# Gated attention then top-1 experts on one core: gates in polar form by scans over time, 96-deep heads, state kept in PSUM, routing by batch into fixed places

## The chip, the cores and the metric

The kernel runs on one NeuronCore of a Trainium2 chip. The metric is device time in microseconds (us), the median of the timed runs. A profiled execution gives, beside it, a span (first to last instruction) and the rows by engine: PE (matrix products), PEld (its weight loads), DVE (VectorE), ACT (ScalarE), POOL (GpSimd), SP (which only issues transfers here).

## What is computed

Two blocks follow each other, all in fp32. The first is a linear attention with a complex gate for each of B = 4 batches, H = 8 heads, S = 768 tokens, head size D = 48; the second sends each of the 3072 tokens to one of 8 experts.

```python
mag = np.sqrt(a_re * a_re + a_im * a_im)
scale = np.minimum(mag, 0.999) / (mag + 1e-06)
a_re_n, a_im_n = (a_re * scale, a_im * scale)
...
for t in range(S):
    new_re = ar * S_re - ai * S_im
    new_im = ar * S_im + ai * S_re
    kv = np.einsum('bhd,bhe->bhde', k[:, :, t], v[:, :, t])
    S_re, S_im = (new_re + kv, new_im)
    y[:, :, t] = np.einsum('bhd,bhde->bhe', q[:, :, t], S_re)
...
logits = x @ w_gate
expert_idx = np.argmax(logits, axis=1)
...
    h = np.maximum(xe @ w1[e], 0.0)
    ye = h @ w2[e]
    out[mask] = gate_w[mask, None] * ye
```

x is y with the heads side by side, 384 wide; w1 is 384 x 1024 and w2 1024 x 384 for each expert; `gate_w` is the softmax probability of the chosen expert.

## The kernel before

**Attention.** The running product P of the gates turns the recurrence into products of matrices: a score is the sum over d of (qP) times (kP / |P|^2) over both parts, within chunks of 128 tokens, and a state carries the rest from chunk to chunk. The work is cut into 16 head pairs (4 batches of 4 pairs), two heads in partitions 0-47 and 64-111, all 768 tokens in the free dimension. For each pair `front` (L217) does `limit` (L72: magnitude by Square and Sqrt on ACT, a reciprocal on DVE), `running` (L104: products within blocks of 8 tokens by 28 DVE instructions, then across 16 blocks by 24 more, then six POOL multiplies, adds and subtracts of 720 elements a partition, L138 to L141) and `factors` (L143: a second reciprocal and the two products qp and kp). `attention` (L160) then makes, per chunk and head, the scores (L170, two 48-deep products, one per part), the mask (L174, DVE), the values (L184) and the part of the state (L187); the new state needs a transpose of kp (L192), a copy on ACT (L194), a product (L198) and four DVE instructions (L202 or L204 to L211). DVE helpers all go by L47.

The order is program order: `ready = front(i + 1)` is issued ahead of `attention(i, ...)` in the loop at L232, so that each engine's queue holds the next pair's gates ahead of this pair's products. After a batch, its rows go to HBM (L237) and their logits are made (L240).

**Check and routing.** L244 to L308 test whether any chunk's product is too small, and hold two loops that run zero times with ordinary gates. L310 to L430 then find, for all 3072 tokens at once, the token of each place in 31 tiles of 128 tokens, each of one expert (`NTILE`).

**Experts.** The loop at L444 gathers for each of the 31 tiles its tokens (L446) and the two weight matrices of its expert (L448, L450) by indirect transfers from POOL, 3.1 MB of weights a tile; then three transposes (L453), 24 products of 128 columns (L460), Relu halves on ACT and DVE (L462, L463), 8 products of 384 columns (L466), the scaling (L468, DVE) and an indirect store of the rows (L469, POOL).

Of the kernel before, what the change touches and what calls it, by code (L numbers as in the profile page):

```python
# [19 lines left out]
C = S // 128            # chunks of 128 tokens in a sequence  # L20
HP = H // 2             # head pairs in a batch
NP = B * HP             # head pairs; head u of a pair lies in partitions 64u..64u+63
HS = (slice(0, 64), slice(64, 128))
HD = (slice(0, D), slice(64, 64 + D))
BK = 8                  # tokens in a block of the running product
NB = 128 // BK
NT = N // 128
DT, FT = DM // 128, F // 128
NTILE = NT + E - 1      # tiles of one expert each: sum of ceil(count / 128) is at most this
W = DM + 1              # a row of x and its gate  # L30
TB = 8                  # tokens in a step of the general path
LEAST = 1e-20           # of |product of a chunk's gates|^2, for the factored form
# [3 lines left out]
def gateloop_then_moe(ctx, tc, q, k, a_re, a_im, v, wg, w1, w2, out):  # L36
    nc = tc.nc
    x_hbm = nc.dram_tensor("x_hbm", (N + 1, W), FP32, kind="Internal").ap()

    consts = ctx.enter_context(tc.tile_pool(name="consts", bufs=1))  # L40
    route = ctx.enter_context(tc.tile_pool(name="route", bufs=1))
# [7 lines left out]
    ident = consts.tile([128, 128], FP32, name="ident")  # L49
    make_identity(nc, ident)  # L50
    causal = consts.tile([128, 128], FP32, name="causal")
    make_upper_triangular(nc, causal, val=1.0, diag=True)
    wgate = consts.tile([128, DT * E], FP32, name="wgate")
    nc.sync.dma_start(wgate, wg)
    zrow = consts.tile([1, W], FP32, name="zrow")
    nc.vector.memset(zrow, 0.0)
    nc.sync.dma_start(x_hbm[N:N + 1, :], zrow)

    lg_all = route.tile([128, NT, E], FP32, name="lg_all")
    good = route.tile([128, NP, C], FP32, name="good")  # L60

    def logits(x, tp_pool, tp_tag, lg, xt_pool):
        """x: 128 tokens' rows; their logits into lg (PSUM)."""
        tp = tp_pool.tile([128, DT, 128], FP32, name="xt_ps", tag=tp_tag)
        for d in range(DT):
            nc.tensor.transpose(tp[:, d, :], x[:, d * 128:d * 128 + 128], ident)
        xt = xt_pool.tile([128, DT, 128], FP32, name="xt")
        nc.scalar.copy(xt, tp)
        for d in range(DT):
            nc.tensor.matmul(lg, lhsT=xt[:, d, :], rhs=wgate[:, d * E:d * E + E], start=(d == 0), stop=(d == DT - 1))  # L70

    def limit(a, sq, mag, den):  # L72
        """Gates a: [128, (re, im), n], in place."""
        nc.scalar.activation(sq, a, func=ACT.Square)
        tt(mag, sq[:, 0, :], sq[:, 1, :], ALU.add)
        nc.scalar.activation(mag, mag, func=ACT.Sqrt)
        nc.vector.tensor_scalar_add(den, mag, 1e-6)
        nc.vector.reciprocal(den, den)  # L78
        nc.vector.scalar_tensor_tensor(out=den, in0=mag, scalar=0.999, in1=den, op0=ALU.min, op1=ALU.mult)
        tt(a, a, bc(den[:, None, :], list(a.shape)), ALU.mult)  # L80

    with ExitStack() as att:
        pool = lambda nm, n, **kw: att.enter_context(tc.tile_pool(name=nm, bufs=n, **kw))
        ld = pool("ld", 3)
        bt = pool("bt", 2)
        big = pool("big", 2)
        tmp = pool("tmp", 1)
        small = pool("small", 2)
        psA = pool("psA", 2, space=PSUM)
        psY = pool("psY", 1, space=PSUM)  # L90
        psT = pool("psT", 1, space=PSUM)
        psG = pool("psG", 1, space=PSUM)

        def load(i):
            a = ld.tile([128, 2, S], FP32, name="a", bufs=4)
            nc.sync.dma_start(a[:, 0, :], a_re[i])
            nc.sync.dma_start(a[:, 1, :], a_im[i])
            qs = ld.tile([128, S], FP32, name="qs")
            ks = ld.tile([128, S], FP32, name="ks")
            nc.sync.dma_start(qs, q[i])  # L100
            nc.sync.dma_start(ks, k[i])
            return a, qs, ks

        def running(a):  # L104
            """In place: products of the gates from each chunk's start to each of its tokens."""
            blk = a.rearrange("p u (n j) -> p u n j", j=BK)
            nb = S // BK
            for j in range(1, BK):
                cur = blk[:, :, :, j]
                u = small.tile([128, 2, nb], FP32, name="u")  # L110
                w = small.tile([128, 2, nb], FP32, name="w")
                tt(u, cur, bc(blk[:, 0:1, :, j - 1], [128, 2, nb]), ALU.mult)
                tt(w, cur, bc(blk[:, 1:2, :, j - 1], [128, 2, nb]), ALU.mult)
                tt(cur[:, 0, :], u[:, 0, :], w[:, 1, :], ALU.subtract)
                tt(cur[:, 1, :], u[:, 1, :], w[:, 0, :], ALU.add)
            t = small.tile([128, 2, nb], FP32, name="t")
            nc.vector.tensor_copy(t, blk[:, :, :, BK - 1])
            m = 1
            while m < NB:
                g = nb // (2 * m)  # L120
                tv = t.rearrange("p u (g r m) -> p u g r m", r=2, m=m)
                prod = {}
                for x in range(2):
                    for y in range(2):
                        z = small.tile([128, nb // 2], FP32, name=f"z{x}{y}").rearrange("p (g m) -> p g m", m=m)
                        tt(z, tv[:, x, :, 1, :], bc(tv[:, y, :, 0, m - 1:m], [128, g, m]), ALU.mult)
                        prod[x, y] = z
                tt(tv[:, 0, :, 1, :], prod[0, 0], prod[1, 1], ALU.subtract)
                tt(tv[:, 1, :, 1, :], prod[0, 1], prod[1, 0], ALU.add)
                m *= 2  # L130
            av = a.rearrange("p u (c n j) -> p u c n j", c=C, j=BK)[:, :, :, 1:, :]
            pv = t.rearrange("p u (c n) -> p u c n", c=C)[:, :, :, :NB - 1]
            shape = [128, C, NB - 1, BK]
            prod = {}
            for x in range(2):
                for y in range(2):
                    z = tmp.tile(shape, FP32, name=f"y{x}{y}")
                    tt(z, av[:, x], bc(pv[:, y, :, :, None], shape), ALU.mult, nc.gpsimd)  # L138
                    prod[x, y] = z
            tt(av[:, 0], prod[0, 0], prod[1, 1], ALU.subtract, nc.gpsimd)  # L140
            tt(av[:, 1], prod[0, 1], prod[1, 0], ALU.add, nc.gpsimd)  # L141

        def factors(i, p, qs, ks):  # L143
            """q P and k P / |P|^2, so that a score is the sum over d of both their parts' products."""
            sq = tmp.tile([128, 2, S], FP32, name="sq", bufs=2)
            nc.scalar.activation(sq, p, func=ACT.Square)
# [13 lines left out]
        def attention(i, p, qp, kp, vb, xb):  # L160
# [3 lines left out]
            for half in range(2):  # L164
# [11 lines left out]
                for cc in range(3):  # L176
# [11 lines left out]
                    if c == C - 1:  # L188
                        continue
# [322 lines left out]
```

## Time and profile before

| | us |
|---|---|
| median of 3 runs (1226.98 to 1228.46) | 1227.65 |
| span of the profiled execution | 1230.5 |
| PE busy in it, 4913 instructions | 912.9 |
| DVE busy, 1564 instructions | 766.0 |
| POOL busy, 237 instructions | 267.4 |
| ACT busy, 219 instructions | 132.6 |

The profile is of an execution of its own, whose only time is its span; all three timed runs lie 2 to 3.5 us below it. A row of a table of groups reads: line, engine, operation, output<-input, partitions x elements, count, then busy us and mean ns of one, then the idle time of the engine ahead of it and what ended that. In a table of stretches each engine's busy us stands with its number of instructions in brackets. The granted clock of TensorE is full nearly throughout, so PE durations compare directly.

### The profile page before, as it was taken

How to read it: one execution, taken by the hardware profiler on the slowest of the kernel's cores; microseconds unless marked ns; L12 is line 12 of the kernel's file. 1: busy time of each engine (PE TensorE's matmuls, PEld its weight loads, DVE VectorE, ACT ScalarE, POOL GpSimd, SP SyncE). 2: the span in 40 equal slices, each digit the busy share in tenths (PEclk: the TensorE clock that was granted, in tenths of full speed). 3: DMA queues.
4: the chain of work that ended last, by engine and by line, in shares of the span. 5: the costliest groups of instructions: out<-in, count | busy, mean ns of one | idle time of the engine just before them, and what ended most of it. 6: DMA issues, size and time to landing. Idle time of an engine off the chain costs nothing. (4 is left out here: it accounts for less than half of the span.)

```text
span 1230.5 us, 12763 instructions
## 1 busy us (share of the span) xinstructions
PE 912.9 (74%) x4913; PEld 737.9 (60%) x4913; DVE 766.0 (62%) x1564; ACT 132.6 (11%) x219; POOL 267.4 (22%) x237
## 2 busy tenths in 40 slices
PE   0286585785775886857779558572899999999998
PEld 0165474674654665645657457562677777777776
DVE  6689899789898879998969889514111111111111
ACT  1111101111101121011020110110000000000000
POOL 0220220202202202112022021101233332433330
PEclk9999999999999999999999999999999999999999
DMA  7010100301101121011020000011877878888880
GB/s 256 26 39 14 52 21 31 129 1 52 39 14 52 32 97 39 14 52 39 13 89 1 0 1 1 1 40 18 360 289 301 335 297 327 330 318 322 322 308 6
DMA packets 31682, 143.84 MB, mean 117 GB/s; under 512 B 6689, under 2 KB 12866, under 8 KB 23682
## 3 DMA queue, kind: packets, MB, share of 16 engines
q0 software_dynamic: 12896, 108.36, 23.1%
q1 hardware_dynamic: 12498, 29.90, 7.3%
q10 hardware_dynamic: 6224, 4.73, 1.2%
q8 instruction: 39, 0.64, 0.2%
q14 instruction: 25, 0.20, 0.0%
HBM read 133.52 MB, written 10.83 MB: 117 GB/s over the span
## 5 line engine op out<-in xcount | busy, mean ns | idle before, releaser
L170 PE MATMUL at<-qp,kp 48*128 48x128 f32 x768 | 127.7, 451 | 206.7 <-DVE kp L47 206.7
L170 PEld LDWEIGHTS at<-qp,kp 48*128 48x128 f32 x768 | 104.1, 320 | 226.1 <-DVE kp L47 208.9
L47 POOL TENSOR_TENSOR y<-a,t 128x720 f32<-128x720 f32 x64 | 89.9, 1436 | 626.4 <-issue 594.8
L187 PE MATMUL y<-st,qp 48*128 48x48 f32 x640 | 180.8, 421 | 27.5 <-DVE st L211 22.7
L187 PEld LDWEIGHTS y<-st,qp 48*128 48x128 f32 x640 | 150.5, 317 | 52.4 <-DVE st L211 27.6
L460 PEld LDWEIGHTS h_ps<-xt,w1t 128*128 128x128 f32 x1488 | 173.7, 194 | 13.0 <-issue 5.0
L460 PE MATMUL h_ps<-xt,w1t 128*128 128x128 f32 x1488 | 174.0, 278 | 4.6 <-DMA w1t<-in_moe_w_dram,widx 4.6
L466 PE MATMUL o_ps<-w2t,ht 128*128 128x384 f32 x496 | 167.9, 492 | 12.4 <-ACT ht L462 11.4
L466 PEld LDWEIGHTS o_ps<-w2t,ht 128*128 128x128 f32 x496 | 91.7, 190 | 76.0 <-ACT ht L462 17.3
L184 PE MATMUL y<-vb,am 128*128 128x48 f32 x384 | 122.1, 426 | 5.2 <-DVE am L47 5.2
L455 DVE COPY xt<-xt_ps 128x384 f32<-128x384 f32 x31 | 17.2, 556 | 153.7 <-PE xt_ps L453 153.7
L184 PEld LDWEIGHTS y<-vb,am 128*128 128x128 f32 x384 | 95.2, 313 | 23.6 <-DVE am L47 7.1
L468 DVE TENSOR_SCALAR yo<-o_ps,xs 128x384 f32<-128x384 f32 x31 | 19.2, 618 | 133.5 <-PE o_ps L466 133.5
L152 DVE RECIPROCAL n<-n 128x768 f32<-128x768 f32 x16 | 79.3, 4953 | 0.5
L78 DVE RECIPROCAL den<-den 128x768 f32<-128x768 f32 x16 | 79.2, 4948 | 0.1
L469 POOL DMA_INDIRECT out_dram<-yo,idx x31 | 31.5, 1016 | 198.7 <-DVE yo L468 197.8
L194 ACT COPY kt<-kt_ps 128x256 f32<-128x256 f32 x80 | 29.8, 372 | 321.8 <-PE kt_ps L192 187.7
L198 PE MATMUL g<-vb,kt 128*64 128x48 f32 x640 | 62.3, 316 | 0.5 <-ACT kt L194 0.5
L192 PE MATMUL kt_ps<-ident,kp 128*128 128x128 f32 x160 | 55.4, 448 | 8.1 <-ACT kt L194 8.1
L211 DVE SCALAR_TENSOR_TENSOR st<-s,a,m 128x48 f32<-128x48 f32 x80 | 61.4, 767 | 0.0
L209 DVE SCALAR_TENSOR_TENSOR st<-s,a,m 128x48 f32<-128x48 f32 x80 | 59.7, 746 | 1.2
L462 ACT ACTIVATE ht<-h_ps 128x512 f32<-128x512 f32 x31 | 18.5, 597 | 361.4 <-PE h_ps L460 314.6
(116 smaller groups left out, 972.0 us busy)
## 6 DMA issues: line engine op xcount, KB each, us to landing
a<-in_a_re_dram SPq DMA_DIRECT2D x16, 384.0 KB, 3.0
a<-in_a_im_dram SPq DMA_DIRECT2D x16, 384.0 KB, 3.8
qs<-in_q_dram SPq DMA_DIRECT2D x16, 384.0 KB, 3.8
ks<-in_k_dram SPq DMA_DIRECT2D x16, 384.0 KB, 3.0
vb<-in_v_dram SPq DMA_DIRECT2D x4, 1152.0 KB, 9.4
x_hbm<-xb ACTq DMA_DIRECT2D x4, 1152.0 KB, 8.6
xs<-x_hbm,idx POOLq DMA_INDIRECT x31
w1t<-in_moe_w_dram,widx POOLq DMA_INDIRECT x31
```

Source lines behind the costliest of these rows:

```text
L47: (eng or nc.vector).tensor_tensor(out=o, in0=a, in1=b, op=op)
L78: nc.vector.reciprocal(den, den)
L152: nc.vector.reciprocal(n2, n2)
L170: nc.tensor.matmul(at[:, h, cc * 128:cc * 128 + 128], lhsT=kp[HD[h], u, sl], rhs=qp[HD[h], u, sl], start=(u == 0), stop=(u == 1))
L184: nc.tensor.matmul(yh, lhsT=am[:, h, cc, :], rhs=val(h), start=True, stop=(c == 0))
L187: nc.tensor.matmul(yh, lhsT=qp[HD[h], u, sl], rhs=st[HD[h], u, :], start=False, stop=(u == 1))
L192: nc.tensor.transpose(kt_ps[:, u, :], kp[:, u, sl], ident)
L198: nc.tensor.matmul(g[HS[h], u, :], lhsT=kt[:, u, HS[h]], rhs=val(h), start=True, stop=True)
L209: nc.vector.scalar_tensor_tensor(out=st[:, 0, :], in0=s0[:, 1, :], scalar=end[1], in1=m[:, 0, :], op0=ALU.mult, op1=ALU.add)
L211: nc.vector.scalar_tensor_tensor(out=st[:, 1, :], in0=s0[:, 0, :], scalar=end[1], in1=m[:, 1, :], op0=ALU.mult, op1=ALU.subtract, reverse1 ...
L460: nc.tensor.matmul(h_ps[:, f, :], lhsT=w1t[:, c:c + 128], rhs=xt[:, d, :], start=(d == 0), stop=(d == DT - 1))
L466: nc.tensor.matmul(o_ps, lhsT=ht[:, f, :], rhs=w2t[:, f * DM:f * DM + DM], start=(f == 0), stop=(f == FT - 1))
```

## The change

Nearly all of the kernel is written anew.

- **Gates.** The inputs are laid out with 128 partitions x 3 groups (all 8 heads of 48 fill 384 rows exactly) by tokens. A *unit* is 384 tokens of one batch, so 1152 elements a partition (the first half of batch 0 is two smaller units of 128 and 256 tokens). The log of the gate's magnitude and its angle are found by Ln, Exp and Arctan on ACT and summed over time by `tensor_tensor_scan` on DVE; Exp and Sin of the sums, times q and k, give qp and kp. Both reciprocals and the block products go. Six multiplies of a unit stand on POOL.
- **96-deep heads.** Transfers from SBUF to SBUF (20 a unit, issued by SP) place a head's real and imaginary rows under each other, so that a score is one 96-deep product.
- **State.** The gates are not rescaled at each chunk, so the state is one sum in a PSUM bank (`ST`), to which each chunk adds; DVE copies it to SBUF after each chunk. Outputs are made transposed (`YT`, two heads in two halves of the output partitions), copied by ACT and turned back with the gate's weights beside (`XT`), which also gives the logits.
- **Routing** is done after each batch: every expert has 448 places in HBM (`xs_hbm`), and POOL stores the rows there by indirect transfers of 128.
- **Experts** run one by one: weights loaded once by SP, 448 columns at a time, and the last 64 places of two experts share one output.
- **Order.** `Plan` takes every step with its engine, an assumed duration and its reads and writes, plays it forward, and the steps are emitted in order of their planned start. Each engine's queue keeps that order. Its engines are taken as independent of each other.
- **Check.** Four tests (angle, decay of a chunk, decay in all, places of an expert) set the counts of the two loops, which now come after the experts.

The core of the gates, of a unit (`fast` is the first unit only; left out after Arctan are three scans of the angle, a tensor_scalar, a scalar_tensor_tensor and a tensor_scalar, all on DVE):

```diff
+            activ(a, a, ACT.Ln, (A,), (A,), "LE", n)
+            activ(c, a, ACT.Exp, (A,), (Ck,), "LE", n, scale=-1.0)
...
+                P.add("POOL", pool_t(n), lambda: tt(im, im, c, ALU.mult, nc.gpsimd), (Bk, Ck), (Bk,))
+            P.add("DVE", dve2(n), lambda: nc.vector.tensor_tensor_reduce(
+                out=c, in0=im, in1=im, scale=1.0, scalar=0.0, op0=ALU.mult, op1=ALU.max, accum_out=chk[:, u:u + 1]),
...
+            activ(c, c, ACT.Ln, (Ck,), (Ck,), "LE", n, bias=one)
+            P.add("DVE", dve2(n), lambda: nc.vector.scalar_tensor_tensor(
+                out=a, in0=c, scalar=0.5, in1=a, op0=ALU.mult, op1=ALU.add), (Ck, A), (A,))
+            activ(c, a, ACT.Exp, (A,), (Ck,), "LE", n, scale=-1.0)
+            activ(c, c, ACT.Ln, (Ck,), (Ck,), "LE", n, scale=1e-6, bias=one)
+            P.add("DVE", dve1(n), lambda: nc.vector.tensor_scalar_min(a, a, LNMAX), (A,), (A,))
+            for g in range(G):
+                P.add("DVE", 2 * T * 0.00104 + 0.08, lambda g=g: nc.vector.tensor_tensor_scan(
+                    d[:, g, :], a[:, g, :], c[:, g, :], lend[:, b, g, c0:c0 + 1], ALU.add, ALU.subtract),
...
+            activ(a, d, ACT.Exp, Dk, (A,), "LE", n, bias=cpos)
+            activ(c, d, ACT.Exp, Dk, (Ck,), "LE", n, scale=-1.0, bias=cneg)
...
+                P.add("POOL", pool_t(n), lambda: tt(qq, qq, a, ALU.mult, nc.gpsimd), (Q, A), (Q,))
+                P.add("POOL", pool_t(n), lambda: tt(kk, kk, c, ALU.mult, nc.gpsimd), (K, Ck), (K,))
+            activ(im, im, ACT.Arctan, (Bk,), (Bk,), "T", n)
...
+            activ(si, si, ACT.Sin, Sk, Sk, "T", n, scale=TWOPI)
+            activ(co, co, ACT.Sin, ("co",), ("co",), "T", n, scale=-TWOPI, bias=hpi)
+            for nm, o, x, xk, eng in (("kp", kp, kk, K, "DVE"), ("qp", qp, qq, Q, "POOL")):
+                for part, key, tr in ((1, Sk, si), (0, ("co",), co)):
+                    e = "DVE" if fast else eng
+                    if nm == "kp" and part == 0 and not fast:
+                        e = "POOL"
```

A chunk and the experts (PE parts):

```diff
+                        nc.tensor.matmul(SC[hf][:, (h % 4) * 128:(h % 4) * 128 + 128], lhsT=hk[slot][:, h, o],
+                                         rhs=hq[slot][:, h, o], start=True, stop=True)
...
+                        nc.tensor.matmul(YT[ps, (h // 2) * 128:(h // 2) * 128 + 128], lhsT=V[:, cl, h * 64:h * 64 + 64],
+                                         rhs=am[2 * par + hf][:, h % 4, :], start=(c == 0 and h < 2), stop=True,
...
+                        nc.tensor.matmul(HB[hb][:, 0:CAP], lhsT=w1b[ws][:, c:c + 128], rhs=xrt[s][:, d, :], start=(d == 0), stop=(d == DT - 1))
...
+                            nc.tensor.matmul(OB[ob][64 * z:64 * z + 64, 0:DM], lhsT=ht[z][:, f_, 384:CAP],
+                                             rhs=w2b[(e - 1 + z) % NW][:, f_ * DM:f_ * DM + DM], start=(f_ == 0), stop=(f_ == FT - 1),
```

## The prediction

> **What bounds the kernel now.** I read the stages first, in the table of stretches cut at the first attention product (54 us), the last pair's kp (786), routing (838) and the experts (866 to 1226).
>
> ```profile
> 0.00:54.00 54.00, 0.00 (x0) 0.00 (x0) 33.77 (x67) 8.59 (x7) 10.05 (x14) 1.00 0.45 158
> 54.00:786.00 732.00, 520.19 (x2592) 425.83 (x2592) 654.13 (x1322) 98.43 (x166) 134.65 (x90) 1.00 0.10 35
> 786.00:838.00 52.00, 43.45 (x218) 36.14 (x218) 8.07 (x30) 5.43 (x13) 1.60 (x4) 1.00 0.07 24
> 838.00:866.00 28.00, 2.87 (x30) 2.21 (x30) 15.33 (x55) 1.65 (x2) 7.80 (x13) 1.00 0.29 88
> 866.00:1226.00 360.00, 346.42 (x2074) 273.67 (x2074) 54.19 (x92) 18.51 (x31) 112.35 (x116) 1.00 0.77 295
> ```
>
> Column three after the stretch is DVE: 654 of 732 us, so DVE sets the attention's pace (48.8 us a head pair); in the experts PE does, 346 of 360. In between, 80 us have one engine or none at work. Then the groups and the timeline gave durations:
>
> ```profile
> L460 PE MATMUL h_ps<-xt,w1t 128*128 128x128 f32 x1488 | 174.0, 278 | 4.6 <-DMA w1t<-in_moe_w_dram,widx 4.6
> L466 PE MATMUL o_ps<-w2t,ht 128*128 128x384 f32 x496 | 167.9, 492 | 12.4 <-ACT ht L462 11.4
> L152 DVE RECIPROCAL n<-n 128x768 f32<-128x768 f32 x16 | 79.3, 4953 | 0.5
> L47 POOL TENSOR_TENSOR y<-a,t 128x720 f32<-128x720 f32 x64 | 89.9, 1436 | 626.4 <-issue 594.8
> ```
>
> Last, why DVE is 89% busy with ever fewer elements: its timeline, and POOL's, in one burst of POOL.
>
> ```profile
> 124.95 0.25 DVE L47 TENSOR_TENSOR s<-g,st 128x96 f32<-128x96 f32 x1
> 125.24 1.32 DVE L207 TENSOR_SCALAR m<-s,a 128x96 f32<-128x96 f32 x1
> 126.59 1.36 DVE L209 SCALAR_TENSOR_TENSOR st<-s,a,m 128x48 f32<-128x48 f32 x1
> 127.87 1.47 DVE L211 SCALAR_TENSOR_TENSOR st<-s,a,m 128x48 f32<-128x48 f32 x1
> 129.45 0.26 DVE L47 TENSOR_TENSOR s<-g,st 128x96 f32<-128x96 f32 x1
> 129.74 1.00 DVE L207 TENSOR_SCALAR m<-s,a 128x96 f32<-128x96 f32 x1
> ```
>
> ```profile
> 125.05 5.62 POOL L47 TENSOR_TENSOR y<-a,t 128x720 f32<-128x720 f32 x4 [38.21 <-issue]
> 130.75 3.36 POOL L47 TENSOR_TENSOR a<-y,y 128x720 f32<-128x720 f32 x2
> ```
>
> L207, L209 and L211 take 0.27 us elsewhere; beside POOL each lasts until a POOL multiply ends. The sum at L47 that reads PSUM (0.25) is not held. DVE's "busy" there is waiting.
>
> [...] Here two L184 instructions between 48-deep ones take 0.59 us, against 0.112 each in the experts; parallel halves are shown by nothing.
>
> **Experts.** Durations from start to start. Last-but-one tile: 48 instructions of L460 from 1202.80 to 1208.16, so 0.112 for 128 columns; 16 of L466 from 1209.01 to 1214.27, so 0.329 for 384, 0.856 ns a column. An fp32 product is two instructions. Per expert: 48 of 448 columns at 0.384 = 18.4 us; three full places of 128, 3 x 5.26 = 15.8; 12 transposes at 0.11 to 0.16, 1.6; together 35.8, times 8 = 286. The shared last places: 4 x 32 instructions x 0.329 = 42 if the halves go one after another, 21 if side by side; I take 26. Stalls: a tile's 11.47 us holds 0.5 beyond its PE work; 0.5 at each of 8 experts, 4. Sum **316 us** (307 to 332), for 360 now. Weights fall from 31 to 8 loads of 3.1 MB, hidden under 39 us of products each; bare, one costs 8.5 us at 372 GB/s (the store of x at 820 us, with rows of 1536 bytes).
>
> **Attention: the shared port.** Per unit of 1152 elements, DVE instructions with two SBUF inputs: 4 at 1.35 (0.947 at 768, 1.75 at 1536) = 5.4; one-input ones, 3 at 0.76 (0.559 at 768, halves per element) = 2.3; 6 scans of 384, at half the rate of such an instruction 0.95, at its full rate 0.55: I take 0.95, 5.7; two small copies 0.3. Sum 13.7 (11.3). POOL's six multiplies: 1.436 at 720 gives 2.30 each, 13.8; the slower form at L140 (1.699) would make 16.3. Together 27.5 us of port (25 to 30), for 8 units' worth **220 us** (201 to 240). [...]
>
> DVE's other work reads PSUM and needs no port: per chunk two masks of 512 at 0.67, state copy 0.68, x copy 0.56, logits 0.2 = 2.8, times 24 = 67; routing some 14 small steps of 0.2, times 4 = 11. Of 78, 11 belong to the tail below. Of the other 67, those hide that stand at the head of DVE's queue while a POOL multiply runs: with some 15 of them and 15 port instructions a unit in mixed order, one or two get through before a port instruction stops the queue, so 48 multiplies x 1.5 x 0.6 = 43. I take two thirds, 45, as hidden and add the rest, **22** (0 if all hide, 67 if none). POOL also gets 24 indirect stores at 1.0 in its queue; 18 lie before the tail and fit into its idle half, 18 more at worst.
>
> Everything else lies beneath. ACT: 10 functions at 1.17, copies 3 x 1.55, two table loads at 1.3 = 19 us a unit, 152. PE per chunk: 8 transposes, 16 score, 32 value and state instructions of 128 columns, 16 of 64, 8 of 104, at 0.112 or less: 6.8 to 8.6[...]; I take 8.3, 200 in all (182 to 245). Transfers: 5.5 MB a unit, a fill of 5.5 and stores of 4.7, 54 MB, 146 us at 372 GB/s[...]. SP: 25 issues a unit at 0.4, 10 us. If the port's cover went, ACT or PE would be next, near 200.
>
> **Ends.** Lead-in: inputs land at 4 to 6 us, the first chain has little beside it: 10. From the last gate product to the first expert product: transfer 4, three chunks x 8.3 = 25, routing 14 steps x 0.3 = 4, six indirect stores at 1.3 apart = 8, landing 2.3 (857 to 860 for a gather), load 3.8, transposes and copies 2: **49**. All of now's 80 us between stages goes with that. After the last product: 4.5 as now; the two empty loops, hidden before (trips at 819.3, PE on at 824.8), are bare now, 5.5: **10**.
>
> Sum: 10 + 220 + 22 + 49 + 316 + 10 = 627 us of span. Now's span is 2.9 above its median; I take 3 off: **624 us**.
>
> **The rivals.** *Engines free of each other* (20%): plans and queues happen to set POOL apart from DVE, or the lock holds less for long instructions. Then DVE's own 13.7 + 8.4 + 1.4 = 23.5 a unit binds: 178 after the tail's share, in place of 242: 560. Against it: six rows held to POOL's very end. *The order does not fit* (18%): the plan counts no lock, so late qp and kp stand in front of other work in SP's and PE's in-order queues. Ten us more a unit: 704. For it: one queue issues both the moves and the next loads; against it: double buffers. *Slower* (1.5%): a test sends the kernel into the token loop, bare at the end. 768 tokens at 10 us at least (some 20 DVE steps at 0.33 and a transfer in and out of 3) add 7.7 ms; it decides once, say, one expert has over 448 tokens. Computed from the inputs, the fullest has 421, the decay sums to -79.6 (limit -100), the angle's squared tangent is 0.28 (2.25). That the change does not do what it says would show so too.
>
> **Numbers.** Forecast 60% (585 to 680). From 560 to 705 about one in ten is left out on each side: half of the first rival, half of the second. Within 0.2% (2.5 us, about what a measurement can tell from no change) would need 600 us of errors: 0.5%.
>
> **What would show it.** DVE instructions on SBUF of 1152 elements lasting well over 1.35 us with a POOL multiply beside, some 30 us a unit; scans near 0.95; expert products at 0.384; some 49 us between the last gate product and the first expert product. Multiplies on both engines at bare durations at once would make it wrong, as would PE busy over 90% in the attention, or an expert beyond 41 us.

## The result, and the profile after

The median is **685.9 us** (683.2 to 689.7, four runs) against 1227.3 for the kernel before on the same chip: a ratio of 0.559, 95% interval 0.557 to 0.561. The profiled execution has a span of 685.5. I cut it at the points of the prediction's sum: POOL's first multiply (39.05), the end of the last gate product (294.35), the first expert product (364.11), the last one's end (669.8). The tail has a further cut at 334, when TensorE has finished the attention. Of the kernels below, e6, e7 and e11 spread over 14 to 17 us from run to run (every other over less than 9), and a ratio takes only the runs within 1.5% of the fastest, which leaves two of four in e6, three in e7 and one in e11.

The stretches of the kernel after; the columns behind the stretch are its length, then busy time of PE, PEld, DVE, ACT and POOL (instructions), the granted TensorE clock, the DMA engines' share, GB/s:

```profile
39.00:295.00 256.00, 163.02 (x1383) 148.74 (x1383) 210.28 (x248) 150.46 (x163) 152.53 (x58) 0.87 0.61 152
295.00:334.00 39.00, 35.33 (x409) 32.59 (x406) 19.93 (x61) 7.87 (x15) 10.54 (x12) 0.99 0.28 82
334.00:364.10 30.10, 3.24 (x15) 2.14 (x15) 2.46 (x17) 0.96 (x2) 7.46 (x9) 0.50 0.74 274
364.10:669.80 305.70, 303.25 (x980) 163.38 (x980) 44.06 (x81) 23.68 (x46) 26.22 (x27) 0.99 0.26 94
669.80:685.50 15.70, 0.00 (x0) 0.00 (x0) 0.60 (x1) 0.00 (x0) 2.03 (x2) 0.65 0.07 26
```

No column is full in the first line: DVE and POOL are busy 210 and 153 of 256 us, and their sum exceeds the stretch. In the second TensorE, busy for 35.3 of 39 us, works off chunks that the gates have left behind; in the third no engine is busy for over a quarter, while the DMA engines are at 0.74. The experts are TensorE's, as before. The clock column counts as full all time ahead of the trace's first clock record, which is at 125.0 us here; by the spacing of the products TensorE had half its clock until then (rows in the last section), which makes the first line's 0.87 some 0.70.

| term of the sum | forecast | measured | difference |
|---|---|---|---|
| lead-in, to POOL's first multiply | 10 | 39.1 | +29 |
| middle (220 port + 22), to the last gate product | 242 | 255.3 | +13 |
| tail, to the first expert product | 49 | 69.8 | +21 |
| experts | 316 | 305.7 | -10 |
| end | 10 | 15.7 | +6 |
| span | 627 | 685.5 | +59 |

**The port.** Two stretches of DVE's timeline in the kernel after, and POOL's beside them:

```profile
203.91 0.66 DVE L389 COPY sb<-bank 96x512 f32<-96x512 f32 x1
204.50 5.96 DVE L297 TENSOR_TENSOR_SCAN cs<-ones_t,tend,B 128x384 f32<-128x384 f32 x2
...
211.30 1.64 DVE L158 TENSOR_TENSOR sub<-lg,mx 128x48 f32<-128x48 f32 x1
...
271.01 1.00 DVE L297 TENSOR_TENSOR_SCAN cs<-ones_t,tend,B 128x384 f32<-128x384 f32 x1
...
277.07 0.67 DVE L158 TENSOR_TENSOR am<-bank,causal 128x512 f32<-128x512 f32 x1
...
277.86 3.04 DVE L305 SCALAR_TENSOR_TENSOR cs<-cs 128x1152 f32<-128x1152 f32 x1
```

```profile
203.13 3.28 POOL L158 TENSOR_TENSOR qp<-Q,cs 128x1152 f32<-128x1152 f32 x1
206.38 3.26 POOL L158 TENSOR_TENSOR B<-B,C 128x1152 f32<-128x1152 f32 x1
209.60 3.27 POOL L158 TENSOR_TENSOR K<-K,C 128x1152 f32<-128x1152 f32 x1
...
277.05 2.63 POOL L158 TENSOR_TENSOR K<-K,C 128x1152 f32<-128x1152 f32 x1 [3.89 <-ACT C L240]
```

At 271 a scan of 384 has no multiply beside it: 1.00 us. At 204.50 two of them last 5.96, because each begins inside a POOL multiply and ends 0.82 us after it: the second at 210.46, its multiply at 209.64. The mask at 277.07, which reads PSUM, keeps its 0.67 beside the same kind of multiply; the two-step product at 277.86 (1.34 bare) does not. POOL is held as well: 2.63 bare, 3.26 to 3.28 with a scan in between. So the two engines take turns here, and a DVE instruction's time is the rest of a multiply plus most of its own. In the whole trace, 32 DVE instructions with two SBUF inputs begin inside a multiply: 30 end after it, and the other two (at 167.81 and 225.55, 1.35 each) have multiplies of 4.41 and 4.81 beside them. Of 43 that read PSUM, 34 end before the multiply does; of 16 with one SBUF input or none, 12. "Port" is the forecast's name for this taking of turns; that it is a port the rows do not show. The forecast's prices of DVE's single steps hold: the scan takes 1.00 bare, against 0.55 for a two-input product of the same 384 (kp of the first unit), so about half its rate, where 0.95 was taken; one-input steps of 1152 (L278, L304) take 0.74 to 0.75 for 0.76.

How much of the middle this fills can be counted in the trace, each instant once. Between 39.05 and 294.36 the port is in use, by DVE on SBUF operands or by a POOL multiply, for 223.6 us; DVE works on PSUM alone for another 18.2; for 13.5 neither works.

**The lead-in.** SP's queue, then POOL's, at the start of the kernel after (for SPq the second column is the time the issue took):

```profile
8.98 0.70 SPq L478 DMA_DIRECT2D xs_hbm<-empty  x1
9.72 16.92 SPq L458 DMA_DIRECT2D wgr<-in_moe_w_gate_dram  x1
26.75 0.69 SPq L258 DMA_DIRECT2D B<-in_a_im_dram  x1
```

```profile
38.88 0.21 POOL L466 COPY turn<-wgr 128x32 f32<-128x32 f32 x1 [32.14 <-DMA wgr<-in_moe_w_gate_dram]
39.05 1.79 POOL L158 TENSOR_TENSOR B<-B,C 128x768 f32<-128x768 f32 x1
```

`setup` asks for the gate weights behind the fill of 5.4 MB, and SP stands 16.9 us in that one issue; then POOL waits 32.1 us for them to build `turn`, with unit 1's multiply queued behind. TensorE first uses `turn` at 122.8.

**The tail.** The last store of rows, the tail's transfer and the experts' start, by the chain of waits of the kernel after:

```profile
343.69 0.97 POOL xs_hbm L450
344.96 11.20 DMA xs_hbm<-xg,slot
356.76 3.93 DMA xr<-xs_hbm
```

Six stores lie 1.28 apart, as forecast (1.3). The last one's landing is 11.2 where I had 2.3.

### The profile page after: what moved, and what is told of

Its sections match the earlier page's. It is cut to its first block, busy times and chain, and to the rows that moved or that the text cites. A ratio compares the mean times of both kernels' runs of the same rounds, so it can differ in the third digit from the quotient of the medians.

```text
span 685.5 us, 7434 instructions
## 1 busy us (share of the span) xinstructions
PE 504.8 (74%) x2783; PEld 346.9 (51%) x2783; DVE 282.2 (41%) x419; ACT 192.7 (28%) x239; POOL 204.7 (30%) x141
## 4 chain that ended last, share of the span: by engine, by line
issue 45%; PE 17%; DVE 16%; DMA 9%; POOL 7%; ACT 2%; SPq 2%; POOLq 0%; DVEq 0%; ACTq 0%
DVE cs L297 6%; PE bank L358 5%; DMA wgr<-in_moe_w_gate_dram 4%; POOL out_dram L537 4%; PE bank L377 3%; PE bank L385 3%; PE bank L393 3%; DVE D L280 2%; PE bank L370 2%; DMA xs_hbm<-xg,slot 2%; PE bank L351 1%; DMA K<-in_k_dram 1%; DVE kp L158 1%; DVE C L270 1%; POOL xs_hbm L450 1%
## 5 line engine op out<-in xcount | busy, mean ns | idle before, releaser
L578 PE MATMUL bank<-xrt,w1b 128*128 128x448 f32 x384 | 148.8, 544 | 2.0 <-ACT xrt L569 2.0
L592 PE MATMUL bank<-w2b,ht 128*128 128x384 f32 x384 | 126.5, 487 | 0.0
L578 PEld LDWEIGHTS bank<-xrt,w1b 128*128 128x128 f32 x384 | 73.0, 192 | 70.9 <-issue 66.3
L592 PEld LDWEIGHTS bank<-w2b,ht 128*128 128x128 f32 x384 | 72.5, 190 | 51.3 <-issue 3.6
L358 PE MATMUL bank<-hq,hk 96*128 96x128 f32 x384 | 62.1, 325 | 12.8 <-issue 7.4
L358 PEld LDWEIGHTS bank<-hq,hk 96*128 96x128 f32 x384 | 57.0, 234 | 17.0 <-issue 11.4
L158 POOL TENSOR_TENSOR qp<-Q,cs 128x1152 f32<-128x1152 f32 (+1 forms) x16 | 49.3, 3089 | 32.4 <-ACT cs L240 16.1
L297 DVE TENSOR_TENSOR_SCAN cs<-ones_t,tend,B 128x384 f32<-128x384 f32 (+2 forms) x27 | 45.5, 1728 | 2.8 <-POOL qp L158 1.8
L385 PE MATMUL bank<-v,kt 128*96 128x64 f32 x320 | 36.5, 277 | 1.4 <-DVE sb L389 1.1
L385 PEld LDWEIGHTS bank<-v,kt 128*96 128x96 f32 x320 | 35.3, 194 | 2.5 <-DVE sb L389 1.3
```

The source lines that it names most:

```text
L158: (eng or nc.vector).tensor_tensor(out=o, in0=a, in1=b, op=op)
L297: P.add("DVE", 2 * T * 0.00104 + 0.08, lambda g=g: nc.vector.tensor_tensor_scan(si[:, g, :], ones_t[:, sl], im[:, g, :], tend[:, b, g, c0: ...
L358: nc.tensor.matmul(SC[hf][:, (h % 4) * 128:(h % 4) * 128 + 128], lhsT=hk[slot][:, h, o], rhs=hq[slot][:, h, o], start=True, stop=True)
L385: nc.tensor.matmul(ST[0:96, h * 64:h * 64 + 64], lhsT=kt[par][:, h * 96:h * 96 + 96], rhs=V[:, cl, h * 64:h * 64 + 64], start=(c == 0 and ...
L578: nc.tensor.matmul(HB[hb][:, 0:CAP], lhsT=w1b[ws][:, c:c + 128], rhs=xrt[s][:, d, :], start=(d == 0), stop=(d == DT - 1))
L592: nc.tensor.matmul(OB[ob][:, 0:DM], lhsT=ht[s][:, f_, j * 128:j * 128 + 128], rhs=w2b[ws][:, f_ * DM:f_ * DM + DM], start=(f_ == 0), stop= ...
```

## The experiments

All ran on the same program text apart from the edit; a small edit of a step also makes `Plan` order other steps anew. Every ratio is to the kernel before, beside it on the same chip. Times in the table are us from the span's start in the profiled execution; the last column is the median of four runs. A row is one execution, up to 6 us from its kernel's median, so a few us between two rows say little by themselves.

| kernel | first attention product | last gate product ends | attention's last product ends | first expert product | span | median |
|---|---|---|---|---|---|---|
| after | 68.2 | 294.4 | 330.8 | 364.1 | 685.5 | 685.9 |
| e1 gate weights first | 55.8 | 276.2 | 317.4 | 350.9 | 671.6 | 675.1 |
| e2 fill late | 48.6 | 284.4 | 321.1 | 354.3 | 676.6 | 682.2 |
| e3 multiplies on DVE | 57.4 | 277.0 | 313.8 | 347.0 | 668.3 | 666.6 |
| e4 weights early | 68.8 | 292.3 | 333.5 | 358.5 | 680.3 | 680.9 |
| e5 = e1 + fill later | 40.4 | 272.5 | 317.6 | 351.0 | 672.7 | 671.8 |
| e6 = e1 + e3 | 55.6 | 274.5 | 316.6 | 349.7 | 670.0 | 666.2 |
| e7 all four | 41.0 | 261.0 | 297.5 | 322.4 | 645.2 | 645.5 |
| e8 = e5, three multiplies out | 41.9 | 258.3 | 300.9 | 334.4 | 655.2 | 653.9 |
| e9 = e5, less TensorE | 40.6 | 268.5 | 303.1 | 336.9 | 657.0 | 658.7 |
| e12 = e7, less TensorE | 40.9 | 264.4 | 294.9 | 320.5 | 641.3 | 640.2 |

**e1: the gate weights first.**

```diff
     wgr = const([128, 56], "wgr")
+    nc.sync.dma_start(wgr, wg)
...
-            nc.sync.dma_start(wgr, wg)
```

> The small load of the gate's weights is issued ahead of all others instead of behind the fill. Theory (POOL stood from 6.7 to 38.9 us for that load, and the attention's port work could not start): POOL's first multiply moves from 39 to about 10 us, and 25 to 29 us go, to about 659. Rival (the transfers of the first 40 us, the fill among them, bound the start anyway, since they run at 250 to 290 GB/s): under 12 us go, because the first units' inputs come late.

Measured: 675.12, ratio 0.5507 (0.5498 to 0.5517), 11 less. POOL's timeline in this kernel:

```profile
10.90 1.80 POOL L158 TENSOR_TENSOR B<-B,C 128x768 f32<-128x768 f32 x1 [3.78 <-ACT C L241]
...
46.46 1.80 POOL L158 TENSOR_TENSOR qp<-Q,cs 128x768 f32<-128x768 f32 x1 [16.40 <-DMA hk<-kp]
```

The wait is gone, the first multiply comes 28 us earlier, and yet later multiplies wait for moves behind the fill. The last gate product ends 18 us earlier, the first expert product comes 13 earlier: TensorE's backlog behind the last gate product grew from 36 to 41 us. The rival holds.

**e2: the fill late.**

```diff
-                if u == 1:
+                if u == 3:
```

The fill then follows the first batch's stores and wipes them, so that batch's rows are missing from the output.

> The fill of the places in HBM (5.4 MB) is planned with the fourth unit instead of the second; the gate's load stays where it is. Theory (the gate's load was late because the fill was queued ahead of it): it lands within some 5 us of its issue, and 20 to 27 us go. Rival (the load is late by its place in the queue and by its 128 short rows, not by the fill): POOL still stands past 25 us and under 10 us go; the fill may cost its time again later.

Measured: 682.17, ratio 0.5574 (0.5552 to 0.5596), 4 less, which the intervals do not part from nothing: the rival's size, though the first attention product came 20 us earlier. POOL's wait shows what the fill was to blame for:

```profile
19.20 0.21 POOL L466 COPY turn<-wgr 128x32 f32<-128x32 f32 x1 [12.42 <-DMA wgr<-in_moe_w_gate_dram]
```

It waits 12.4 us in place of 32.1, so the fill is some 20 of them. The rest is there without it: the theory's landing within 5 us of the issue (at 8.41) did not come, nor did the rival's stand past 25. Whether the load's short rows make it late, no run shows.

**e3: all multiplies on DVE.**

```diff
-            fast = u == 0
+            fast = True
...
-                P.add("POOL", pool_t(n), lambda: tt(kk, kk, c, ALU.mult, nc.gpsimd), (K, Ck), (K,))
+                P.add("DVE", dve2(n), lambda: tt(kk, kk, c, ALU.mult), (K, Ck), (K,))
```

> All six multiplies of a unit go from POOL to DVE, which frees POOL and gives DVE 6 x 1.35 = 8.1 us a unit more. Theory (DVE and POOL exclude each other, so what counts is the sum: 13.7 + 6 x 2.63 = 29.5 us of port now, 21.8 then, beside 8.4 + 1.4 us of PSUM work that can no longer hide): 31.6 us a unit, the stretch of 255 us between the first POOL multiply and the last gate product stays within 15 us of that; POOL no longer stands in the way of the first unit either, so the whole is 15 to 35 us faster. Rival (engines free of each other, DVE's own work set the pace): DVE's load rises from 23.5 to 31.6, 65 us more in that stretch, 30 to 60 us slower in all. Scans at 1.0 us each wherever they stand, by the first.

Measured: 666.56 (662.4 to 671.0), ratio 0.5425 (0.5389 to 0.546), 19 less: inside the theory's 15 to 35, where the rival had 30 to 60 more. DVE's busy time is 280.7 us with 49 more multiplies on it, against 282.2 without: at 1.35 each for the 42 full ones, and less for seven smaller, it would be some 63 us more for all 49. As much of DVE's "busy" in the kernel after had been waiting for the port. But this edit also takes unit 1's multiply out from behind `turn`, so part of the 19 may be e1's gain; e6, with the gate weights first, takes that out.

**e4: the experts' weight buffers early.** The check's block, unchanged, is moved behind the allocation of the experts' buffers.

```diff
-    with ExitStack() as fs:
-        fp = fs.enter_context(tc.tile_pool(name="chkp", bufs=1, reuse_waits="tile"))
...
         TP, HB, OB = bank[0:2], bank[2:5], bank[5:8]
+        with ExitStack() as fs:
+            fp = fs.enter_context(tc.tile_pool(name="chkp", bufs=1, reuse_waits="tile"))
```

> The experts' buffers are placed ahead of the check's small tiles, so that the first weights do not wait for the check and load during the last chunks. Theory (the last stores and the first x load took 11.2 and 3.9 us beside 4.7 MB of weights): the weights land before 335, stores and x go unhindered, 8 to 14 us go. Rival (the stores land late on their own, POOL's six issues at 1.28 and their completion): under 3 us go.

Measured: 680.9, ratio 0.5545 (0.5517 to 0.5572), 5 less: between the two. The weights now leave at 300 us, and the first row transfer of the experts, on ACT's queue as before, follows the last store (347.75) after 3.3 us in place of 11.8:

```profile
351.08 0.40 ACTq L554 DMA_DIRECT2D xr<-xs_hbm  x1
```

From the last store to the first expert product it is 10.7 us against 19.2, 8.5 less. The last gate product ends 2 earlier, but TensorE's backlog grew from 36 to 41, so that 6 are left at the first expert product.

**e5: e1, and the fill behind unit 2's first scans.**

```diff
-                if u == 1:
+                if u == 2:
...
-                        (), ("empty",), lat=2, kb=5500)
+                        (("lend", 0, 6),), ("empty",), lat=2, kb=5500)
```

> The gate weights are asked for first, as in the run with that edit alone (675.1), and the fill of the places (5.4 MB) is planned behind unit 2's first scans, so still ahead of every store of rows. Theory that the transfers of the first 40 us bound the start: the fill's 18 to 19 us of DMA time leave it, PE's first product comes 10 to 18 us earlier than the 55.8 of that run, and the median is 657 to 666. Rival: the start is bound by the chain of ACT, DVE and POOL work of the first units, not by the transfers: 672 to 680.

Measured: 671.76, ratio 0.5471 (0.5462 to 0.548), 3 less than e1. The theory was right on the first attention product (40.4, 15 earlier) and wrong on what that is worth: the last gate product ends at 272.5, 4 earlier than in e1, and the backlog grows by the same 4. The start of TensorE hardly moves the end of the gates. The rival's number is nearer but not its reason: had the first units' own chain bound the start, 55.8 would have stayed.

**e6: e1 and e3 together.**

> The gate weights first, and all six multiplies of a unit on DVE, so POOL's multiplies are gone in the middle and the late gate weights can't be what is saved. Theory that DVE and POOL share a port and POOL is the worse place for this work (2.63 a multiply against 1.35 on DVE): 8 to 18 faster than the run with the gate weights alone (675.1), so 657 to 667. Rival: what the run with the multiplies on DVE won (666.6 against 685.9) was its start, since its first multiply no longer stood behind POOL's wait for the gate weights: 672 to 680 here, no gain over the gate weights alone.

Measured: 666.17 with a wide spread (657.5 to 671.8), ratio 0.5383 (0.5351 to 0.5414) from the two shorter runs (657.5 and 664.0). The median of all four is 9 below e1's, the mean of those two 14, and all four lie below e1's fastest (673.4): the theory's 8 to 18 holds, and e3's gain was not its start alone. How e3's 19 divides is not shown, since gains do not add here. The profiled execution is the longest of the four, and in it the last gate product ends only 1.7 earlier than in e1. Whether the gain is the port or POOL's longer multiply in each unit's chain, this run leaves open.

**e7: all four edits.**

> Gate weights first, the fill behind unit 2's first scans, the multiplies on DVE, and the experts' weight buffers placed before the check's small tiles. Theory that the four costs are separate: 685.9 less 11 (gate), 8 to 18 (fill), 8 to 18 (multiplies), 5 (weights): 634 to 654. Rival: they are one and the same wait at the start, seen four times, and the end of the attention stage is bound elsewhere: 658 to 667, no better than the best so far.

Measured: **645.46**, ratio 0.5245 (0.5235 to 0.5256), the fastest version with the whole computation. It lies within the theory's 634 to 654; yet one by one the four gave 11, 3, 9 to 14 and 5, 28 to 33 in all, and together 40. It is 26 below e5: the last gate product 11.5 earlier, the backlog 36.6 for 45, the way from the last store 10.7 for 19.3. Its stretches say what binds once POOL has no multiplies:

```profile
40.00:80.00 40.00, 24.06 (x136) 21.71 (x138) 39.76 (x48) 35.65 (x35) 0.00 (x0) 1.00 0.77 199
80.00:100.00 20.00, 8.12 (x84) 7.38 (x80) 7.61 (x12) 9.93 (x10) 0.00 (x0) 0.82 0.99 226
...
160.00:200.00 40.00, 32.89 (x334) 28.86 (x334) 36.57 (x52) 23.93 (x27) 0.00 (x0) 0.94 0.67 177
...
240.00:261.00 21.00, 17.81 (x193) 16.15 (x191) 20.54 (x36) 10.76 (x14) 0.00 (x0) 1.00 0.16 42
```

DVE is full at 40 to 80 and at 240 to 261, and nearly so from 160 to 200, now at bare durations. Between 80 and 100 no engine is busy for half of the time: DVE waits 12.4 us for a load of q and ACT 8.8 for one of a_re, with the DMA engines at 0.99. The fill, issued at 63.7, has a part in that (in e5 one took 24.8 us to land), the moves of q and k and the loads have the rest.

**e8: e5 with three of POOL's multiplies left out of each unit** (those of `im`, `qq` and `kk`; all three by the same edit).

```diff
-                P.add("POOL", pool_t(n), lambda: tt(im, im, c, ALU.mult, nc.gpsimd), (Bk, Ck), (Bk,))
+                P.add("POOL", pool_t(n), lambda: None, (Bk, Ck), (Bk,))
```

> As the run with gate weights first and the later fill, but POOL's three in-place multiplies of each unit (a_im by 1/|a|, q and k by their decays; two of them in the first unit, k's alone) are left out, and the count of the general path is set to zero; the output is not the reference's. POOL keeps one product of k and both of q. Theory that the DVE and POOL port bounds the middle: three multiplies of 2.63 over seven units and a third, about 55 us of port time, go, and the median falls by 35 to 55 against the run with the two edits. Rival: PE at its lowered clock and the moves of q and k between partitions bound the middle: 0 to 15 less.

Measured: 653.9, ratio 0.5323 (0.5314 to 0.5332), 18 less than e5. POOL's busy time falls by 76 us (208.0 to 132.3), and the last gate product ends 14 earlier. Less of this work does end the gates earlier, but another limit stands about 14 us behind it; I had expected 35 to 55. From the first attention product to the last gate product DVE or a POOL multiply is at work for 218.0 of 232.1 us in e5 and for 178.9 of 216.4 here: 39 us of work are gone, and 23 of them have become time in which neither works. DVE's longest waits here are 21.9 us in all for scores of TensorE (9.7 in e5) and 9.0 for ACT. The edit also takes three steps out of each unit's chain, so it does not part the shared port from POOL's place in that chain; for the port stand the rows held in turn and the count above.

**e9: e5 with TensorE's state products out.**

```diff
-                        nc.tensor.matmul(YT[ps, (h // 2) * 128:(h // 2) * 128 + 128], lhsT=sb[1 - par][0:96, h * 64:h * 64 + 64],
-                                         rhs=hq[slot][:, h, o], start=(h < 2), stop=False, skip_group_check=True)
+                        pass
...
-                    for h in range(H):
+                    for h in range(H if c == 0 else 0):
```

> As the run with the gate weights first and the later fill (671.8), but TensorE's products of the state with q are left out, and the state's update in every chunk but a batch's first; the count of the general path is set to zero, and the output is not the reference's. That takes some 55 to 65 us of TensorE's busy time out of the attention stage, as much as the earlier run took off POOL's (which gave 18). Theory that TensorE at its lowered clock bounds the middle together with the port: 15 to 35 less, and the last six chunks behind the last gate product shrink from 44 to under 33. Rival, the port alone: 0 to 8 less, all of it in those last chunks.

Measured: 658.65, ratio 0.5365 (0.5356 to 0.5373), 13 less: between the theories, and the place tells more than the size. Of it 4 us lie before the last gate product and 10 in the backlog (45 to 35). TensorE sets the tail, not the middle.

**e10: e7 with TensorE's gaps filled** by nine more products a unit.

```diff
+        def idle(x, key, T):
+            def f():
...
+                    nc.tensor.matmul(RT[:, 128:128 + T], lhsT=ident, rhs=x[:, g, :], start=True, stop=True)
+            P.add("PE", 0.7, f, key, ())
...
+            idle(im, (Bk,), T)
+            idle(c, (Ck,), T)
```

> As the run with all four edits (645.5), with nine more TensorE products of one 128x384 slice for each unit, each of a tile that the gates have just made, into part of the routing's bank that nobody reads; they fill TensorE's gaps. Theory that TensorE's granted clock falls to a half after gaps in its work and comes back after some 10 us without one: the mean clock between 80 and 280 us goes from about 0.81 to over 0.92 and the time falls by 3 to 15, though nearly 50 us of work are added. Rival, the clock follows the load of the whole core: it stays under 0.85, and the added work shows as 10 to 30 more.

Measured: 663.5, ratio 0.5409 (0.5381 to 0.5438), 18 more. The clock between 80 and 280 us did rise, from 0.81 to 0.90, against both texts in part: higher than the rival's bound, short of the theory's. The 18 do not price the added products: 8.7 lie before the last gate product (269.7 for 261.0), and 8.7 more between the attention's last product and the last store (22.9 for 14.2). There the last batch's `slot` waits for the stores of the batch before it, which here land beside the experts' weights, issued at 306 to 307 (in e7 from 271 on). The same step in the kernel after, in e7 and in e10:

```profile
337.61 0.20 DVE L443 TENSOR_REDUCE slot<-z 128x6 int32<-128x48 f32 x1 [3.58 <-DMA xs_hbm<-xg,slot]
```

```profile
304.28 0.20 DVE L444 TENSOR_REDUCE slot<-z 128x6 int32<-128x48 f32 x1 [3.46 <-DMA xs_hbm<-xg,slot]
```

```profile
322.73 0.20 DVE L459 TENSOR_REDUCE slot<-z 128x6 int32<-128x48 f32 x1 [12.15 <-DMA xs_hbm<-xg,slot]
```

Inconclusive on the clock's cause.

**e11: e7 with the fill in four quarters.**

```diff
-                if u == 2:
+                for z, key in {0: ((0, 1),), 1: ((1, 3),), 2: ((2, 6), (3, 6))}.get(u, ()):
...
-                        (("lend", 0, 6),), ("empty",), lat=2, kb=5500)
+                        (("lend", 0, key),), (("empty", z),), lat=2, kb=1375)
```

> As the run with all four edits (645.5), with the fill cut in four quarters of 1.4 MB, one behind the first scans of units 0 and 1 and two behind those of unit 2. Theory that the fill in one piece keeps the moves of q and k waiting (DMA engines full from 80 to 120 us there, TensorE waiting 20 us in all for k's moves): 3 to 10 less. Rival, the order absorbs it: within 3 of 645.5.

Measured: 653.8, but the four runs lie between 640.8 and 657.4, so that no interval is given and nothing follows. Whether the fill's hole in e7 can be closed stays open.

**e12: e7 with e9's cut.**

> As the run with all four edits (645.5), with the same TensorE products left out as in the run that took TensorE's work off the kernel with POOL's multiplies (which gave 13, of which 4 lay before the last gate product); the count of the general path is zero, and the output is not the reference's. Theory that TensorE at its lowered clock is the next bound once the multiplies have left POOL: the last gate product comes 10 to 25 earlier than the 261 of that run, and the time falls by 20 to 40. Rival, the gates' own chain through ACT, DVE and the moves of q and k is next: the last gate product comes within 6 of 261, and the time falls by 8 to 14, all in the chunks behind it.

Measured: 640.19, ratio 0.5206 (0.518 to 0.5231), 5 less. From the first attention product to the last gate product, e7 and then e12:

```profile
41.00:261.00 220.00, 169.50 (x1446) 151.23 (x1446) 185.19 (x255) 136.09 (x150) 10.91 (x7) 0.84 0.73 184
```

```profile
41.00:264.00 223.00, 145.80 (x982) 128.40 (x982) 184.65 (x254) 135.70 (x149) 9.12 (x7) 0.74 0.71 181
```

A third of TensorE's instructions is gone and the gates end no earlier: the rival's place holds, its size (8 to 14) was too high. The clock is lower, 0.74 for 0.84 as shown, 0.66 for 0.75 with half taken ahead of the first records (77.3 and 82.5), which may give part of the saving back. DVE's 185 us are the same in both.

## Why the forecast held in direction and fell short by 62 us

At 685.9 the kernel lies outside the 585 to 680 that the forecast gave its own mechanism, inside the 560 to 705 around it, and nearer to the second rival's 704 than to 624. The mechanism of the middle is the forecast's all the same; the 62 us are mostly in the lead-in and the tail, and the experts, 10 under, hide part of what was missed.

**The shared port: mechanism right, time in which neither works put at nothing.** The rows above show the two engines in turn, e8 shows that less work on POOL ends the gates earlier, and e9 and e12 that less on TensorE does so by 4 us or not at all. The sum itself came out: 223.6 us of port for 220, 18.2 of PSUM work alone for 22, so 241.8 for 242. The 13 over are the 13.5 us in which neither engine works, a term that the sum does not have; during 12.4 of them ACT does. That the sum was met so closely is partly luck. "1.436 at 720 gives 2.30 each" scaled a duration to 1152, and the multiply takes 2.63: the 49 of them come to 122 us bare where 110 were forecast. What is left of the 223.6 for DVE is 101, where 110 were forecast. Nor does the routing stand clear of the port, as I had it: `sub` at 211.30 reads SBUF, begins inside a POOL multiply and lasts 1.64 for a bare 0.21. ACT came out as priced, busy for 150 us of the middle where 152 were forecast: Ln, Exp, Arctan and Sin of 1152 elements all take 1.16 to 1.17, and 1.25 with a bias tile. The forecast's one rate for all functions had only Square at 1536 (1.48 and 1.49) and Sqrt at 768 (0.84) to rest on, which by themselves do not show it. What the forecast got wrong as well is the room beneath: it put ACT or PE "next, near 200", but with 76 us of POOL's work gone (e8) the stretch from TensorE's start still takes 216, and with none there (e7) 220. In e7 DVE itself is the limit for most of that, with the PSUM work and the multiplies at 185 of 220; in e8 it is not settled, with waits for TensorE's scores and for ACT in DVE's queue.

**The lead-in: the step that failed.** "The first chain has little beside it" looked at the gates alone and not at the queues. SP's fill went ahead of a small load that POOL waited for, with the multiplies queued behind. By the table this cost 29, but e1 takes the wait away and wins 11, and e5 frees the start altogether and wins 14. A late start is partly made up: the terms of such a sum are not independent where two pipelines (gates, TensorE) run behind each other. Of what the gates gained (18 us in e1, 22 in e5), 13 in both reached the experts, and the backlog lost the rest.

**The tail: three terms, each with its run.** TensorE's backlog was "three chunks x 8.3 = 25" and 4 for the transfer, and took 36.4. A chunk costs less than I had, but more were left: by 295 us scores stood for 19 of 24 chunks (304 of 384 L358 instructions) and 17 were turned back (136 of 192 at L393). e9 moves this term, by 10. Routing and stores took 14.2 for 12, and 14.2 to 14.7 in every kernel of the table; 3.6 of it is the wait of `slot` for the stores of the batch before, which the forecast put at nothing. From the last store to the first expert product it was 19.2 for 8.1 (landing, load, transposes): 4.7 MB of expert weights, issued at 339 to 340, moved beside the rows, with the DMA engines at 0.83 and 334 GB/s from 343.69 to 360. e4, e7 and e12 have it at 10.7 or 10.8 with the weights sent earlier, so 8.5 of that 11 is their doing; the other 2.6 is open.

**The experts: better by 10.** Groups of this stage by form, in the kernel after:

```profile
L578 PE MATMUL bank<-xrt,w1b 128*128 128x448 f32 x384 | 148.8, 544 | 2.0 <-ACT xrt L569 2.0
L592 PE MATMUL bank<-w2b,ht 128*128 128x384 f32 x384 | 126.5, 487 | 0.0
L607 PE MATMUL bank<-w2b,ht 128*64 128x384 f32 x128 | 21.5, 489 | 0.0
```

Forecast were 147, 126 and 26, and 4 of stalls. The prices of the two large groups hold to 1%. Each of the first two groups is 48 instructions an expert, two to a product. The column halves run side by side: 128 instructions of L607 in 21.5 us, 0.168 each where one of L592 takes 0.329, which is the lower bound that I had given (21). Stalls are 2.0. The transposes, 12.8 in the forecast, are the other half of the gain: they take 6.5 of this stretch's 303.25 us of PE, and the first expert's lie ahead of it, where the sum had counted them a second time.

**The end: 6 over.** The last store takes 4.4 as forecast; from POOL's memset (674.2) on, the two empty loops take 11.3, twice my 5.5. No run leaves them out, so that is read from one trace only.

**The rivals.** "Engines free of each other" (560) is out by the rows that wait for a multiply's end. "The order does not fit" (704) named the right organ for the lead-in, SP's in-order queue, but not the place: not a unit's moves in front of loads (31.9 us a unit, for 30.3 forecast) but one issue, the fill before the gate weights. The weights beside the last rows are another matter: the rows go by POOL's and ACT's queues and the weights by SP's, so it is not the order in one queue that held the rows; e4 shows that it was the weights (8.5 us), and no run shows by what. So that its sum lies near the result is not this mechanism's doing. The token loop stayed empty.

## What to carry to other kernels

Price two engines that take turns, as DVE and POOL do here on two-input work in SBUF (two scans 5.96 us for 2.00 bare), as a sum, but take the duration of the slower one from its own size, leave room for time in which neither works, and look for the next limit by a count of all work, not of the shared work alone. Read the first 40 us of every in-order queue for a large transfer ahead of a small one that something waits for, and place the next stage's large loads before the last small stores, not beside them. A stage that starts late and a backlog behind it are not two costs to add: test what an earlier start really moves at the far end.

## What was not expected of the hardware

- TensorE's granted clock moves between full and half: the records of both kernels' traces are 1.00 or 0.50, 16 of them in the kernel after and 2 before. The profile has no record of it ahead of its first change, at 871.7 us in the kernel before and at 125.0 in the kernel after, and shows 1.00 for that time. The products say otherwise. Sixteen instructions of scores in the kernel after, ahead of the first record, where 0.50 is recorded, and where 1.00 is:

```profile
69.49 3.67 PE L358 MATMUL bank<-hq,hk 96*128 96x128 f32 x16
...
215.91 3.78 PE L358 MATMUL bank<-hq,hk 96*128 96x128 f32 x16
...
296.54 2.00 PE L358 MATMUL bank<-hq,hk 96*128 96x128 f32 x16
```

  They start 213 ns apart in the first two and 112 in the third. In the kernel before, the instructions of the first expert tile start 213 ns apart up to the record and 112 from there on, those of the last-but-one 112 throughout:

```profile
865.88 8.36 PE L460 MATMUL h_ps<-xt,w1t 128*128 128x128 f32 x48 [4.65 <-DMA w1t<-in_moe_w_dram,widx]
...
1202.80 5.52 PE L460 MATMUL h_ps<-xt,w1t 128*128 128x128 f32 x48
```

  So the kernel before was not at full clock nearly throughout: up to the record these rows put it at half, its attention too, as no change is recorded there, and PE durations of the two kernels do not compare as they stand. The prediction's 0.59 us for two L184 instructions, set beside the experts' 0.112, holds half clock as well; the 0.112 does not.

  With half taken ahead of the first record, the clock between 80 and 280 us is 0.72 in the kernel after, 0.68 in e5. Stretches of 8 us of the kernel after:

```profile
172.00:180.00 8.00, 4.12 (x44) 3.87 (x40) 8.00 (x3) 2.93 (x5) 8.00 (x3) 0.98 0.60 157
180.00:188.00 8.00, 2.12 (x17) 1.57 (x17) 8.00 (x9) 2.83 (x4) 3.92 (x2) 0.50 0.60 149
188.00:196.00 8.00, 7.76 (x72) 7.27 (x72) 7.97 (x13) 5.65 (x8) 1.78 (x1) 0.88 0.99 305
196.00:204.00 8.00, 8.00 (x86) 7.12 (x87) 6.77 (x8) 7.71 (x9) 8.00 (x4) 1.00 0.75 150
...
244.00:252.00 8.00, 8.00 (x56) 7.59 (x54) 5.50 (x14) 2.40 (x3) 5.91 (x3) 0.50 0.70 195
```

  Here 0.50 comes in the second of two stretches with few products, and the clock is back within some 8 us of steady work. That is no rule: between 244 and 252 PE is busy throughout at 0.50, and in the attention of the kernel before it was busy for 520 of 732 us. More work on TensorE in e10 went with a higher clock (0.81 to 0.90 between 80 and 280), less in e12 with a lower one (0.68 there), but e9, with a third of TensorE's instructions gone, has the clock of e5. From the first attention product to the last gate product, e5 and then e9, with first records at 70.3 and 70.6:

```profile
40.40:272.50 232.10, 175.18 (x1309) 157.38 (x1310) 198.80 (x216) 132.04 (x143) 143.69 (x51) 0.73 0.71 173
```

```profile
40.60:268.50 227.90, 130.11 (x877) 115.93 (x878) 200.59 (x216) 131.77 (x143) 142.25 (x51) 0.72 0.73 176
```

  What the clock depends on stays open.
- An issue on SP's queue behind a 5.4 MB fill took 16.9 us, and blocked all later ones. In e1 another load stood there and its issue took 12.45; in e2, without the fill ahead, the gate weights' took 2.16.
